# Turning one more head pair's queries and keys by transposing transfers, and loading both heads in one transfer

## The chip, the cores and the metric

The kernel runs on one core of a Trainium2 chip. The metric is the device time in microseconds. Before the change it is 984.49 us, the median of 3 runs (984.35 to 984.61); the profiled execution spans 983.0 us.

## The reference

The computation is a routed attention, and behind it a feed-forward block. There are 4 batches and 8 heads; a head has 768 rows of queries, keys and values with 64 elements each, and 16 centroids.

```python
q_assign = np.argmax(np.einsum('bhsd,hcd->bhsc', q_n, c_n), axis=-1)
k_assign = np.argmax(np.einsum('bhsd,hcd->bhsc', k_n, c_n), axis=-1)
mask = q_assign[:, :, :, None] == k_assign[:, :, None, :]
scores = scale * np.matmul(q, k.transpose(0, 1, 3, 2))
scores = np.where(mask, scores, -1000000000.0)
...
attn_out = np.matmul(softmax(scores), v)
x = attn_out.transpose(0, 2, 1, 3).reshape(B * S, H * D)    # 3072 x 512
out = np.maximum(x @ w_in, 0.0) ** 2 @ w_out                # d_ff = 2048
```

A query attends only to the keys of its own cluster. The norms of queries and keys don't change an argmax, so the kernel leaves them out and normalizes the centroids alone.

## The kernel before

Heads are worked in pairs: pair number 4 b + hp holds heads 2 hp and 2 hp + 1 of batch b, one in partitions 0 to 63 of a turned tile, the other in 64 to 127. There are NG = 16 pairs, HP = 4 to a batch. Each pair has two halves of 384 queries, and each half has six chunks of 128 keys, taken two at a time. So a **unit** is (pair, half, two chunks), three units to a half. The list `units` puts the first halves of pairs 0 to 3 first (units 0 to 11), then the second halves of pairs 0 to 3 (units 12 to 23), then pair by pair both halves of the other twelve pairs (units 24 to 95).

For the scores, queries and keys must lie with the 64 elements of a head along partitions: tile `qkT`, 128 partitions x 12 chunks x 128 columns. There are two ways to get there:

- `turn(pair, part)`, used for pairs 0 to 3: four 128x128 transposes on TensorE (line 256) for each of three parts, each part copied out of PSUM by ScalarE (line 258). The raw tile has both heads of a row side by side, as the transposes need it: [128, 6 chunks, 2 x 64].
- words, used for pairs 4 to 15: `split_words` has ScalarE copy the 32-bit elements as two planes of 16-bit halves into `flat` (line 277, two copies for queries and two for keys), SyncE writes them to DRAM (`words`, line 278), and `turn_words` reads them back with one transposing transfer (line 288) that fills `qkT`.

Behind `qkT` come `logits` (four products with the centroids on TensorE, a copy `lgs` on ScalarE), `route` (three transposes `lt`, then the argmax by five steps on VectorE, lines 340 to 349) and, for pairs of batch 0, `turn_onehot`: the one-hot cluster codes are transposed on TensorE (`po`, line 382) and copied by ScalarE (`ohT`, lines 390 and 392). In batch 0 the mask is added to the scores by products with these one-hot codes (`sc<-ohT`); in other batches VectorE applies it behind the exponential (line 470).

`prep(pair)` is the list of these steps. It is appended to the list `ahead` at the first unit of the pair before (at unit 16 for pair 4), and each unit takes three entries off it; None holds a place. For pairs of batch 0 the list is turn, turn, turn, logits, route, one-hot, one-hot. For the others it begins with `turn_words` and two empty places, and it also holds the two `split_words` steps of the next pair. Pair 4's own split stands at units 12 and 14.

`load_qk` loads queries and keys of a pair: for each of the two, one transfer for each head, on SyncE's queue (for pair 0 the second head's on ScalarE's). A transfer writes pieces of 256 bytes, 768 of them. The pool `loads` with four buffers serves the raw tiles and `flat`. A pair is loaded when `turn(pair - 2, 2)` has been emitted for pairs 2, 3 and 4, and by `split_words` for pairs from 5 on.

In the same stretch of time the two weight matrices are fetched (`w_raw`, 32 transfers of 512 KB, line 139) and rounded in steps of ScalarE, VectorE and GpSimd (lines 150 to 166), four weight pieces for every three units. The products of the feed-forward block for batch 0 (`ph`, `po` with `gT`) are filled in between the units as soon as batch 0's attention is there.

The sums of the exponentials end in `r` (line 551), go to DRAM (`far_r`) and come back to all partitions (`rb`, line 558), where VectorE multiplies them into `xT` (line 570).

Each engine works through its own queue in order. The programming layer orders instructions by priority and its own estimate of when they can run, so a line's place in the program is not always its place in a queue. SyncE's queue holds nearly all transfers: a transfer that must wait holds up all behind it.

Of the kernel before, what the change touches and what calls it, by code (L numbers as in the profile page):

```python
# [8 lines left out]
F32 = mybir.dt.float32  # L9
BF16 = mybir.dt.bfloat16  # L10
I32 = mybir.dt.int32
U16 = mybir.dt.uint16
# [6 lines left out]
P = 128  # L19
# [6 lines left out]
def kernel(  # L26
# [10 lines left out]
    nc = tc.nc  # L37

    B, H, S, D = q.shape
    C = centroids.shape[1]  # L40
    NCH = S // P
# [4 lines left out]
    HP = H // 2  # L46
# [13 lines left out]
    loads = ctx.enter_context(tc.tile_pool(name="loads", bufs=4))  # L60
    loads_v = ctx.enter_context(tc.tile_pool(name="loads_v", bufs=2))
    qktp = ctx.enter_context(tc.tile_pool(name="qktp", bufs=2))
# [9 lines left out]
    qkt_early = early.enter_context(tc.tile_pool(name="qkt_early", bufs=HP - 2, side="right"))  # L72
# [8 lines left out]
    def bank(name, shape):  # L81
        return ps_f.tile(shape, F32, name=name, tag="f")

    def first_bank(name, shape, dtype=F32):

        return ps_av.tile(shape, dtype, name=name, tag="av")

    def together(products, offset=2000):

        products = iter(products)  # L90
        last = nc.tensor.matmul(**next(products))  # L91
        with tc.high_priority(offset=offset):
            for product in products:
                last = nc.tensor.matmul(**product)  # L94
        return last.ins


    raw = {}
    raw_v = {}

    def load_qk(pair):
        if pair >= NG:
            return
        b, hp = divmod(pair, HP)
        raw[pair] = []
        for name, src in (("q_raw", q), ("k_raw", k)):
            t = loads.tile([P, NCH, 2 * D], F32, name=name, tag="qk")
            for e in range(2):
                (nc.scalar if pair == 0 and e else nc.sync).dma_start(
                    t[:, :, D * e : D * (e + 1)],  # L110
                    src[b, 2 * hp + e].rearrange("(p j) d -> p j d", p=P),
                )
            raw[pair].append(t)
# [15 lines left out]
    for fr in range(DFF // NW):  # L129
        for a in range(KT):  # L130
            cols = slice(fr * NW, (fr + 1) * NW)
# [37 lines left out]
    cen = once_early.tile([P, D], F32, name="cen")  # L169
    nc.scalar.dma_start(cen, centroids.rearrange("h c d -> (h c) d"))  # L170
    load_qk(0)
    load_qk(1)

    ident = const.tile([P, P], F32, name="ident")
# [3 lines left out]
    for _ in range(8):  # L178
# [14 lines left out]
        out=odd[:, 1:2], in0=row_i, scalar1=1.0 / C, scalar2=None, op0=ALU.mult  # L193
    )
    constants = nc.vector.tensor_scalar(
        out=odd[:, 0:1], in0=odd[:, 1:2], scalar1=-1.0, scalar2=1.0, op0=ALU.mult, op1=ALU.add
# [48 lines left out]
    qkT = {}  # L245
# [3 lines left out]
    def turn(pair, part):  # L249
        if part == 0:  # L250
            pool = qkt_early if 2 <= pair < HP else qktp
            qkT[pair] = pool.tile([P, 2 * NCH, P], F32, name="qkT")
        pt = bank("pt", [P, 4, P])
        for i in range(4):
            which, c = divmod(4 * part + i, NCH)
            nc.tensor.transpose(out=pt[:, i], in_=raw[pair][which][:, c], identity=ident)
        dst = qkT[pair][:, 4 * part : 4 * part + 4]
        nc.scalar.copy(out=dst, in_=pt)
        if part == 2:
            raw.pop(pair)  # L260
            if pair in (0, 1, HP - 2):
                load_qk(pair + 2)


# [4 lines left out]
    def split_words(pair, which):  # L269
        if which == 0:  # L270
            words[pair] = dram.tile([2 * NCH, P, 2, 2 * D], U16, name="words")
        flat = loads.tile([P, NCH, 2, 2 * D], U16, name="flat", tag="qk")
        src = raw[pair][which].bitcast(U16).rearrange("p c (d two) -> p c two d", two=2)
        half = NCH // 2
        with tc.issue_after(last_exp[0]):
            for cols in (slice(0, half), slice(half, NCH)):
                nc.scalar.copy(out=flat[:, cols], in_=src[:, cols])
        nc.sync.dma_start(
            words[pair][NCH * which : NCH * (which + 1)].rearrange("c p two d -> p c two d"),
            flat,  # L280
        )
        if which == 1:
            raw.pop(pair)
            load_qk(pair + 1)

    def turn_words(pair):
        qkT[pair] = qktp.tile([P, 2 * NCH, P], F32, name="qkT")
        nc.sync.dma_start(
            qkT[pair].rearrange("p c n -> p (c n)").bitcast(U16),
            words.pop(pair).rearrange("c p two d -> (c p two) d"), transpose=True,  # L290
        )
# [4 lines left out]
    def logits(pair):  # L296
        hp = pair % HP
        lg = (bank if pair else first_bank)("lg", [P, TB])
        last_logits[pair] = together(
            dict(  # L300
                out=lg[32 * g : 32 * g + 32], lhsT=cnT[:, 2 * C * hp : 2 * C * (hp + 1)],
                rhs=qkT[pair][:, NB * g : NB * (g + 1)], start=True, stop=True,
            )
            for g in range(4)
        )
        lgs[pair] = once.tile([P, TB], F32, name="lgs")
        nc.scalar.copy(out=lgs[pair], in_=lg)

    def route(pair):
        with tc.high_priority(offset=2000) if pair <= HP else ExitStack():  # L310
            number(pair)
# [51 lines left out]
    def turn_onehot(pair, which):  # L363
        if pair == 0:

            pt = first_bank("po", [P, 2, NB, P], BF16)
            for i in range(2):
                for c in range(NB):
                    nc.tensor.transpose(
                        out=pt[:, i, c], in_=oh[:, c, 2 * i + which].rearrange("p e c -> p (e c)"),  # L370
                        identity=ident_b,
                    )
            dst = qid[pair][1][:, :, TB * which : TB * (which + 1)]
            src = pt.rearrange("p i c n -> p i (c n)")
            nc.vector.tensor_copy(out=dst[:, 0], in_=src[:, 0])
            nc.scalar.activation(
                out=dst[:, 1], in_=src[:, 1], func=ACT.Copy, bias=-BIG, scale=BIG
            )
            return
        pt = ps_f.tile([P, NCH, P], BF16, name="po", tag="f")  # L380
        for c in range(NCH):
            nc.tensor.transpose(
                out=pt[:, c],
                in_=oh[:, c % NB, 2 * which + c // NB].rearrange("p e c -> p (e c)"),
                identity=ident_b,
            )
        dst = qid[pair][1][:, which]
        src = pt.rearrange("p c n -> p (c n)")
        if which == 0:
            nc.scalar.copy(out=dst, in_=src)  # L390
        else:
            nc.scalar.activation(out=dst, in_=src, func=ACT.Copy, bias=-BIG, scale=BIG)

    def spread(pair):

        src, dst = qid[pair]
        n = 4 * NB
        pb = ps_f.tile([n, P], BF16, name="pb", tag="f")
        nc.tensor.transpose(out=pb, in_=src.rearrange("p g e i -> p (g e i)"), identity=ident_b)
        row = once.tile([n, P], BF16, name="row", tag="b")  # L400
        nc.scalar.copy(out=row, in_=pb)
        far = dram.tile([n, P], BF16, name="far")
        nc.sync.dma_start(far, row)
        nc.sync.dma_start(
            dst.rearrange("p g e n -> p (g e n)"),
            far.rearrange("r n -> (r n)").partition_broadcast(P),
        )

    def prep(pair):
        if pair < HP:  # L410
            return [
                lambda: turn(pair, 0), lambda: turn(pair, 1), lambda: turn(pair, 2),
                lambda: logits(pair), lambda: route(pair),
                lambda: turn_onehot(pair, 0), lambda: turn_onehot(pair, 1),
            ]

        split = [lambda i=i: split_words(pair + 1, i) for i in range(2 if pair + 1 < NG else 0)]
        first, second = split or (None, None)
        return [
            lambda: turn_words(pair), None, None, first, None, None,  # L420
            lambda: logits(pair), None, lambda: route(pair), second, None, None,
            None, None, lambda: spread(pair),
        ]
# [367 lines left out]
    for u in range(len(units) + 2):  # L791
        if u < len(units):
            pair, h, c = units[u]
            if (p := next_pair(u)) is not None:
                ahead.extend(prep(p))
            if u in (TWOS, TWOS + 2):

                split_words(HP, int(u > TWOS))
            if c == 0 and u + 3 < len(units) and units[u + 3][0] not in raw_v:
                load_v(units[u + 3][0])  # L800

            with behind_first(u):
                scores(pair, h, c)
# [9 lines left out]
        while v_next < min(ready, len(units)):  # L813
            pair, h, c = units[v_next]
# [19 lines left out]
        while rounding >= 3:  # L834
            rounding -= 3
            i = next(to_round, None)
# [261 lines left out]
```

## Time and profile before

| engine | busy us | share of the span |
| --- | --- | --- |
| TensorE | 962.6 | 98% |
| VectorE | 562.4 | 57% |
| GpSimd | 376.9 | 38% |
| ScalarE | 315.4 | 32% |

Busy time is the time in which an engine worked on an instruction; shares don't add up, since engines work side by side. The DMA engines' mean busy share, in tenths for 40 equal slices of the span, is 9666572534546345452310 and then nothing above 0: they are loaded to about 60% in the first 150 us, to about half until 450 us, and little after. They move 127575 packets, 74.32 MB; 90906 of the packets are under 512 bytes. Of the groups that the change touches, the 24 transposes of queries on TensorE (and as many of keys) take 272 ns each as the median, the 12 copies out of PSUM 591 ns, the 48 copies into `flat` 816 to 857 ns, and a transposing transfer occupies SyncE's queue for 2.6 to 5.3 us.

### The profile page before, as it was taken

The numbers are of one execution on the slowest core, as the hardware profiler recorded it, in microseconds if no ns is written. First come the engines' busy times: TensorE is split into PE (matmuls) and PEld (weight loads), VectorE is DVE, ScalarE is ACT, GpSimd is POOL, SyncE is SP. The second block draws the span as 40 slices with busy tenths as digits, with TensorE's granted clock in tenths as the row PEclk, the third lists the DMA queues.
The fourth block names the chain that finished last, engine by engine and source line by source line (L and its number), as shares of the span: only waits on it lengthen the run. The fifth ranks groups of instructions, "written<-read, shape, count | busy, mean of one in ns | idle before, by whom it ended". The sixth has DMA issues, their size and how long they took to land.

```text
span 983.0 us, 12011 instructions
## 1 busy us (share of the span) xinstructions
PE 962.6 (98%) x4455; PEld 552.8 (56%) x4455; DVE 562.4 (57%) x913; ACT 315.4 (32%) x510; POOL 376.9 (38%) x277
## 2 busy tenths in 40 slices
PE   7999989999999999999999999999999999999997
PEld 4544444443344444443343555888556888556886
DVE  5777778766566665667654865532566531656331
ACT  5886755444445545544231111000111000111000
POOL 1336666655656556565666231002231002231000
PEclk9999999999999999999999999999999999999999
DMA  9666572534546345452310000000000000000000
GB/s 248 199 186 177 164 212 76 136 108 106 135 111 156 98 109 123 111 142 75 74 42 16 15 0 1 11 22 22 11 1 1 21 22 22 1 0 1 22 22 24
DMA packets 127575, 74.32 MB, mean 76 GB/s; under 512 B 90906, under 2 KB 118934, under 8 KB 127510
## 3 DMA queue, kind: packets, MB, share of 16 engines
q1 hardware_dynamic: 125798, 73.06, 28.1%
q8 instruction: 37, 0.61, 0.3%
q10 hardware_dynamic: 1712, 0.43, 0.2%
q14 instruction: 28, 0.23, 0.1%
HBM read 48.07 MB, written 15.86 MB: 65 GB/s over the span
## 4 chain that ended last, share of the span: by engine, by line
PE 81%; DVE 6%; DMA 5%; issue 3%; ACT 1%; POOL 1%; SPq 1%; ACTq 0%; DVEq 0%; POOLq 0%
PE bank L707 22%; PE bank L676 22%; PE po L597 7%; PE ph L584 6%; PE sc L91 6%; PE sc L94 5%; PE av L91 5%; PE av L94 4%; DMA rb<-far_r 3%; DVE w_raw L162 1%; DVE r L551 1%; PE sm L91 1%; DVE ex L470 1%; DMA far_r<-r 1%; POOL w_in L166 1%
## 5 line engine op out<-in xcount | busy, mean ns | idle before, releaser
L482 POOL TENSOR_TENSOR acc<-acc,ex 128x768 f32<-128x768 f32 x112 | 207.1, 1849 | 115.0 <-DVE ex L470 98.4
L470 DVE SCALAR_TENSOR_TENSOR ex<-qid,ids,sc 128x384 f32<-128x384 bf16 x288 | 157.7, 608 | 63.3 <-ACT sc L466 45.6
L466 ACT ACTIVATE sc<-sc 128x768 f32<-128x768 f32 x144 | 108.5, 792 | 162.1 <-PE sc L94 144.6
L94 PE MATMUL sc<-qkT 64*128 64x384 f32 x576 | 153.4, 505 | 0.7
L94 PE MATMUL av<-ex,v_raw 128*64 128x384 f32 x576 | 136.9, 495 | 0.0
L665 POOL TENSOR_TENSOR w_s<-w_in 128x256 f32<-128x256 f32 x24 | 18.3, 762 | 279.9 <-PE bank L707 162.0
L646 DVE TENSOR_TENSOR g<-bank,g 128x384 f32<-128x384 f32 x144 | 77.9, 556 | 81.5 <-PE bank L676 80.5
L707 PE MATMUL bank<-w_out,g 128*128 128x256 f32 x432 | 95.2, 379 | 0.0
L584 PE MATMUL ph<-xT,w_in 128*128 128x384 f32 x256 | 91.8, 498 | 3.3 <-DVE best L341 2.3
L597 PE MATMUL po<-w_out,gT 128*128 128x512 f32 x192 | 92.7, 615 | 0.0
L91 PE MATMUL sc<-qkT 64*128 64x384 f32 x192 | 87.9, 538 | 2.6 <-DVE ex L470 2.6
L707 PEld LDWEIGHTS bank<-w_out,g 128*128 128x128 f32 x432 | 82.1, 190 | 11.8
L646 DVE TENSOR_TENSOR osb<-bank,osb 128x256 f32<-128x256 f32 x54 | 22.1, 423 | 107.6 <-PE bank L707 102.2
L94 PEld LDWEIGHTS sc<-qkT 64*128 64x128 f32 x576 | 65.4, 187 | 28.6 <-issue 6.7
L91 PE MATMUL av<-ex,v_raw 128*64 128x384 f32 x192 | 81.0, 504 | 0.0
L676 PE MATMUL bank<-xT,w_in 128*128 128x384 f32 x192 | 69.9, 487 | 0.0
L676 PE MATMUL bank<-x_t,w_s 128*128 128x384 f32 x192 | 69.8, 486 | 0.0
L676 PE MATMUL bank<-xT,w_s 128*128 128x384 f32 x192 | 69.8, 486 | 0.0
L584 PEld LDWEIGHTS ph<-xT,w_in 128*128 128x128 f32 x256 | 45.6, 189 | 42.7 <-issue 16.0
L94 PEld LDWEIGHTS av<-ex,v_raw 128*64 128x64 f32 x576 | 49.8, 137 | 34.6 <-issue 34.4
L480 POOL TENSOR_TENSOR acc<-ex 128x768 f32<-128x768 f32 x28 | 51.0, 1822 | 46.9 <-DVE ex L470 39.0
L707 PE MATMUL bank<-w_t,g_s 128*128 128x256 f32 x288 | 65.1, 379 | 0.0
(128 smaller groups left out, 1222.8 us busy)
## 6 DMA issues: line engine op xcount, KB each, us to landing
words<-flat SPq DMA_DIRECT2D x24, 384.0 KB
w_raw<-in_moe_w_in_dram SPq DMA_DIRECT2D x16, 512.0 KB
w_raw<-in_moe_w_out_dram SPq DMA_DIRECT2D x16, 512.0 KB
v_raw<-in_v_dram SPq DMA_DIRECT2D x20, 384.0 KB
q_raw<-in_q_dram SPq DMA_DIRECT2D x31, 192.0 KB
k_raw<-in_k_dram SPq DMA_DIRECT2D x31, 192.0 KB
rb<-far_r SPq DMA_DIRECT2D x62, 96.0 KB
out_dram<-osb SPq DMA_DIRECT2D x23, 256.0 KB
```

Source lines behind the costliest of these rows:

```text
L91: last = nc.tensor.matmul(**next(products))
L94: last = nc.tensor.matmul(**product)
L466: last_exp[0] = nc.scalar.activation(out=t[:, 2 * i : 2 * i + 2] if pair < HP else src, in_=src, func=ACT.Exp, scale=SCALE).ins
L470: nc.vector.scalar_tensor_tensor(out=t[:, 2 * i + e], in0=qid[pair][1][:, h, e], scalar=ids[pair][:, ch % NB, 2 + ch // NB, e : e + 1], in ...
L480: nc.gpsimd.tensor_tensor(out=acc[pair, h], in0=t[:, 0:2], in1=t[:, 2:4], op=ALU.add)
L482: nc.gpsimd.tensor_tensor(out=acc[pair, h], in0=acc[pair, h], in1=t[:, 2 * i : 2 * i + 2], op=ALU.add)
L584: nc.tensor.matmul(ph, lhsT=w_in[:, kk, f * P : (f + 1) * P], rhs=xT[b, h][:, kk], start=(kk == 0), stop=(kk == KT - 1),)
L597: nc.tensor.matmul(po, lhsT=gT[f][:, i * P : (i + 1) * P], rhs=w_out[:, f], start=(f == 0), stop=(f == FT - 1),)
L646: nc.vector.tensor_tensor(out=out, in0=bank, in1=to, op=ALU.add)
L665: nc.gpsimd.tensor_tensor(out=s1, in0=a[1][0], in1=a[1][1], op=ALU.add)
L676: nc.tensor.matmul(bank, lhsT=operands[j][0][:, kk], rhs=operands[j][1][:, kk], start=(kk == 0), stop=(kk == H2 - 1),)
L707: nc.tensor.matmul(bank, lhsT=operands[j][0][:, f], rhs=operands[j][1][:, f], start=(f == 0), stop=(f == F2 - 1),)
```

## The change

Pair 3, the last of batch 0, gets its `qkT` by words and a transposing transfer too, and no longer by transposes on TensorE. Its split steps are put into pair 2's `prep`, between routing and one-hot steps; its own `prep` begins with `turn_words` and two empty places. This takes pair 3's transposes and their copies from TensorE and ScalarE.

From pair 3 on no raw tile has to hold both heads of a row side by side, so the raw tile becomes [128, 2 heads, 6 chunks, 64], and one transfer loads both heads of queries, another both heads of keys, in pieces of 1536 bytes. The side-by-side layout is then made by the copies into `flat`, which are split by head in place of by chunk. The loads of pairs 3 to 15 become fewer transfers with longer pieces. The turned tile of pair 3 is still taken from the early pool.

```diff
         for name, src in (("q_raw", q), ("k_raw", k)):
+            if pair > HP - 2:
+                t = loads.tile([P, 2, NCH, D], F32, name=name, tag="qk")
+                heads = src[b, 2 * hp : 2 * hp + 2]
+                nc.sync.dma_start(t, heads.rearrange("h (p j) d -> p h j d", p=P))
+                raw[pair].append(t)
+                continue
             t = loads.tile([P, NCH, 2 * D], F32, name=name, tag="qk")
...
-            if pair in (0, 1, HP - 2):
+            if pair < 2:
                 load_qk(pair + 2)
...
-        src = raw[pair][which].bitcast(U16).rearrange("p c (d two) -> p c two d", two=2)
-        half = NCH // 2
+        src = raw[pair][which].bitcast(U16).rearrange("p e c (d two) -> p e c two d", two=2)
         with tc.issue_after(last_exp[0]):
-            for cols in (slice(0, half), slice(half, NCH)):
-                nc.scalar.copy(out=flat[:, cols], in_=src[:, cols])
+            for e in range(2):
+                nc.scalar.copy(out=flat[:, :, :, D * e : D * (e + 1)], in_=src[:, e])
...
-        qkT[pair] = qktp.tile([P, 2 * NCH, P], F32, name="qkT")
+        pool = qkt_early if pair < HP else qktp
+        qkT[pair] = pool.tile([P, 2 * NCH, P], F32, name="qkT")
...
     def prep(pair):
-        if pair < HP:
-            return [
-                lambda: turn(pair, 0), lambda: turn(pair, 1), lambda: turn(pair, 2),
-                lambda: logits(pair), lambda: route(pair),
-                lambda: turn_onehot(pair, 0), lambda: turn_onehot(pair, 1),
-            ]
         split = [lambda i=i: split_words(pair + 1, i) for i in range(2 if pair + 1 < NG else 0)]
         first, second = split or (None, None)
+        onehot = [lambda: turn_onehot(pair, 0), lambda: turn_onehot(pair, 1)]
+        turned = [lambda: logits(pair), lambda: route(pair)]
+        if pair < HP - 1:
+            turned = [lambda i=i: turn(pair, i) for i in range(3)] + turned
+            return turned + ([first, *onehot, second] if pair == HP - 2 else onehot)
+        if pair < HP:
+            return [lambda: turn_words(pair), None, None, *turned, *onehot]
```

## The prediction

> **What bounds the kernel now.** I read the table of busy time first, then what TensorE waits for, then the stage that the change touches, queue by queue in order of time.
>
> ```profile
> PE 962.6 (98%) x4455; PEld 552.8 (56%) x4455; DVE 562.4 (57%) x913; ACT 315.4 (32%) x510; POOL 376.9 (38%) x277
> ```
>
> ```profile
> PE sc L91 <- DVE ex L470: 2.6, 3, 1.1
> ...
> PE ph L584 <- DVE best L341: 2.3, 1, 2.3
> ...
> PE ph L584 <- DVE xT L570: 0.8, 1, 0.8
> ```
>
> The first fence is the page (busy us, share of the span); the second is the list of waits (us in total, times, longest). TensorE (PE) is the bound: it idles 20 us of 983. So a change that hides transfers or frees another engine has at most these small waits to win, and whatever makes TensorE wait where it did not is lost outright, because its queue is in order and no later stage has idle time to give back.
>
> The stage concerned is the first halves of batch 0 (about 15 to 75 us), where a pair takes 16 us: units 0 to 11 are pairs 0 to 3, three units each. In the timeline of TensorE and ScalarE (start, duration, engine, instruction):
>
> ```profile
> 48.37 0.87 PE L256 MATMUL pt<-ident,q_raw 128*128 128x128 f32 x6
> ...
> 51.21 0.66 PE L256 MATMUL pt<-ident,k_raw 128*128 128x128 f32 x4
> ...
> 62.49 0.49 PE L94 MATMUL sc<-ohT 64*128 64x384 bf16 x4
> ```
>
> ```profile
> 43.98 0.71 ACT L152 ACTIVATE w_raw<-w_raw 128x512 f32<-128x512 uint32 x1
> 44.89 0.80 ACT L390 COPY ohT<-po 128x768 bf16<-128x768 bf16 x1 [0.20 <-PE po L382]
> ...
> 73.14 1.58 ACT L277 COPY flat<-q_raw 128x768 uint16<-128x768 uint16 x2
> ```
>
> The reader is to see pair 3's transposes on TensorE (six at 48.37, two of k behind them, four at 51.21), its first masked scores at 62.49, and that ScalarE had 0.20 us to spare before the one-hot copy of pair 2. The SyncE queue, and windows of the transfers:
>
> ```profile
> 51.21 1.15 SPq L558 DMA_DIRECT2D rb<-far_r  x2
> ...
> 138.09 3.39 SPq L288 DMA_TRANSPOSE qkT<-words  x1
> ...
> 223.28 4.21 SPq L288 DMA_TRANSPOSE qkT<-words  x1
> ```
>
> ```profile
> 130.00:140.00 10.00, 9.27 (x40) 4.23 (x41) 5.47 (x6) 3.57 (x6) 4.58 (x3) 0.83 0.85 223
> ...
> 228.50:229.00 0.50, 0.50 (x2) 0.19 (x1) 0.34 (x1) 0.00 (x0) 0.50 (x1) 1.00 0.81 177
> 229.00:229.50 0.50, 0.50 (x3) 0.19 (x1) 0.00 (x0) 0.00 (x0) 0.50 (x2) 1.00 0.01 1
> ```
>
> The last three columns of a window are granted clock, DMA share and GB/s. The transposing transfer issued at 223.28 keeps the DMA engines busy until 229.0: 5.7 us from issue, of which 4.2 occupy the SyncE queue. In 130 to 140 the clock is 0.83: it follows the 2.28 us wait that ended at 130.73, and costs 10 x 0.17 = 1.7 us more.
>
> **What the Trainium skill says.** DMA: Bandwidth & Descriptors, Latency and other measured facts, gives transposing transfers 261 GB/s; 128 x 1536 x 4 bytes = 786 KB would take 3.0 us (an estimate from the page), the trace shows 5.7, so I use the trace. The same page, Two DMAs through the same engine are not ordered, says that a transfer that reads what an earlier one writes must wait for its completion on the issuing queue; the trace agrees in the 1.7 us that SyncE once waited for words ahead of a transpose. Specifications there asks for pieces of 512 bytes or more for full rate; the q and k loads are 256-byte pieces now (the page counts 90906 packets under 512 B), but the trace shows only 1.2 us of TensorE time waiting for these loads, at the start. TensorE: Matmul & The Clock Gate, Part 1, says that an idle window of about 3.4 us halves the clock; here 2.28 us already brought a slow stretch.
>
> **The change part by part.**
>
> Removed: 12 transposes on TensorE. By starts, 48.37 to 49.40 and 51.21 to 51.80: 1.03 + 0.59 = 1.62 us, on the bound. Three copies L258 of 0.59 us on ScalarE, hidden.
>
> Added on ScalarE: four flat copies; two take 1.58 us from the row above, or 1.45 by starts. The rows become 12 runs of 64; same element count, so I take the same time. The pair for q falls into ScalarE's idle 1.71 us before the exponential at 40.81: nothing. The pair for k is queued directly ahead of pair 2's one-hot copies. These had 0.20 us to spare, so they start 1.45 - 0.20 = 1.25 us later, and TensorE's masked products of unit 6 (46.51 before) with them. This eats 1.25 of the 1.62 us.
>
> Added transfers: two writes of words and one transpose. Here lies the new wait. In the order in which the changed program queues SyncE's instructions, the write of k's words stands behind the two rb transfers, which end at 52.36, and these hang on pair 1's sums, not on anything that the change speeds up. So it issues at about 52.4. A words write alone (458.57) kept the DMA engines busy until 461.0, 2.4 us; under load the one at 133.22 let its transpose start at 138.09, 4.9 us. The transpose thus starts between 54.8 and 57.3 and lands some 6 us later (5.7 above, 6.5 for the one at 466.94 beside a broadcast): between 60.8 and 63.3; I take 62.
>
> Who waits: TensorE's logits of pair 3, which the changed order puts right after pair 2's sums. TensorE gets there at 58.2: unit 6's masked products at 47.76, 1.86 to unit 7, 1.81 and 1.44 for its scores and products with v, 1.82 and 1.44 for unit 8, 2.09 for the sums (all by starts of before). It idles 3.8 us, with everything behind it: pair 3's scores, two products with v, the masked scores. Then comes the routing chain, which before ran beside scores, v products and 2.1 us of sums: logits 0.8, copy 0.6, transposes 0.6, five VectorE steps 3.0 (56.43 to 59.4), one-hot transposes 0.8, two copies 1.5: 7.3 us. Masked scores of unit 9 at 62 + 7.3 = 69.3. Before they came at 62.49 with two products with v still to do, 2 x 1.44: 65.4. Lag 3.9 us (2.7 to 5.2 with the landing); it already contains the saved transposes. The idle time should cost a slow clock: 1.7 us at 130, of which part falls into the chain's own waits; I take 1.2 (0 to 1.7). Sum: +5.1.
>
> Loads of pairs 3 to 15: 26 transfers of 256 packets for 52 of 768. On SyncE two loads took 1.28 us, v_raw, of the new shape, 0.39: 26 x 0.9 = 23 us off a queue that is mostly idle. The rb transfers of the later stage move up by 0.6 us, since no load stands ahead of them. VectorE waits 56.8 us for rb in all, but TensorE only 2.6 us for VectorE in 150 to 500. I take -0.5 (0 to -2.6). TensorE's 0.8 us at 82 for xT should go, as VectorE does pair 3's 384-wide reciprocal at once after a late sum: -0.8. The 2.3 us wait at 128 stays: VectorE's lateness there starts with rb at 111.7, behind a weight load that waits for GpSimd; nothing of that is touched. Placing pair 3's tile in the early pool costs nothing.
>
> **Forecast**: 984.49 + 5.1 - 0.5 - 0.8 = 988.3 us. Chance 0.58.
>
> **Rivals.**
> - *Nearly even* (0.17): the transpose lands at 60.8, lag 2.7, no clock dip, and the later waits give back 0.8 + 1.3: 985.1. For it: a lone words write needs only 2.4 us. Against: weight and k loads are in flight (DMA share 0.66 in 50 to 60).
> - *Faster* (0.20): the wait at the logits is met because the write issues earlier than the SyncE order suggests or its neighbours wait less. Then 1.62 - 1.25 = 0.4 is kept, the 0.8 at 82 and 2.3 of the 2.6 later go: 984.49 - 3.5 = 981.0. For it: these waits exist and the DMA share is 0.5 in 250 to 450. Against: the write would have to issue by 49.8 (58.2 less 6 less 2.4), ahead of sums that end at 44.4 plus reciprocal and two transfers.
> - *Worse* (0.05): SyncE, held 4.2 us by the transpose, also delays v and the next weights, and the stall at 128 grows: 994.
>
> The slow end of the main case is 5.2 + 1.7 = 6.9, 991.4. Range 982 to 992: it leaves out most of the faster case and the worst. Faster by over 0.2% (below 982.5) 0.2; within it 0.17; slower (above 986.5) 0.63.
>
> **What would show it.** TensorE waiting 2.5 to 5 us at pair 3's logits (L91, lg) for a DMA near 58 us, then a clock below 1.0 in 60 to 70; one-hot copies of pair 2 starting about 46.1; the write of k's words near 52.4 and the transpose at 55 to 57; masked scores of unit 9 at 68 to 71; fewer than 60,000 packets under 512 B (90906 less 52 x 768 = 39,936, plus those of one more transpose); no gain over 2.6 us after 150. Wrong if the logits wait under 1 us, or if the 128 us stall vanishes.

## The result, and the profile after

| kernel | median us (lowest to highest) | ratio to before, 95% interval |
| --- | --- | --- |
| before | 984.55 (983.53 to 984.82) | |
| changed | 991.73 (988.48 to 994.27) | 1.0073 [1.0051, 1.0094] |
| changed, a second time (before: 984.29) | 990.2 (988.59 to 991.86) | 1.0063 [1.0045, 1.0082] |

The change makes the kernel slower by about 7 us in one session and 6 in the other; 988.3 was forecast. The profiled execution of the changed kernel is the fastest of the first six, 988.48 us, with a span of 986.7 us against 983.0 before. So its trace shows less of the loss than the median has.

The page, first the busy line of the engines, then the packets:

```profile
PE 963.9 (98%) x4443; PEld 552.1 (56%) x4443; DVE 564.4 (57%) x913; ACT 316.1 (32%) x511; POOL 375.8 (38%) x277
...
DMA packets 98552, 75.89 MB, mean 77 GB/s; under 512 B 53691, under 2 KB 89911, under 8 KB 98487
```

TensorE has 12 instructions less, as it should, and yet is busy 1.3 us longer: a busy TensorE is not one at full clock. Packets under 512 bytes fell from 90906 to 53691. The list of what TensorE waits for (us in total, times, longest):

```profile
PE lg L91 <- DMA qkT<-words: 4.2, 1, 4.2
PE sc L91 <- DVE ex L477: 2.4, 1, 2.4
...
PE ph L591 <- DVE best L347: 2.3, 1, 2.3
...
PE sc L94 <- ACT ohT L398: 0.9, 1, 0.9
```

The first line is the new wait at pair 3's logits, for the transposing transfer. The third is the stall at 128 us, unchanged. The last is pair 2's one-hot copy, late behind the flat copies. The second stands near 472 us, and was not foreseen. TensorE's timeline around the new wait (start, duration, engine, line, instruction, idle time before it):

```profile
46.57 0.50 PE L94 MATMUL sc<-ohT 64*128 64x384 bf16 x4 [0.92 <-ACT ohT L398]
...
54.95 2.16 PE L94 MATMUL sm<-ex,ups 128*32 128x192 f32 x48
...
61.32 0.51 PE L91 MATMUL lg<-qkT,cnT 128*32 128x384 f32 x1 [4.21 <-DMA qkT<-words]
...
63.90 0.90 PE L323 MATMUL lt<-ident,lgs 128*128 128x128 f32 x3
...
69.53 0.84 PE L388 MATMUL po<-ident_b,oh 128*128 128x128 bf16 x12
71.75 0.50 PE L94 MATMUL sc<-ohT 64*128 64x384 bf16 x4
```

The logits start at 61.32 after 4.21 us of nothing; the masked scores of unit 9, which came at 62.49 before, come at 71.75. SyncE's queue shows why the words are late:

```profile
49.52 1.14 SPq L565 DMA_DIRECT2D rb<-far_r  x2
50.76 0.53 SPq L283 DMA_DIRECT2D words<-flat  x1
...
54.94 4.24 SPq L294 DMA_TRANSPOSE qkT<-words  x1
```

The second write of words goes out behind the two rb transfers, and the transfer starts 4.2 us after it, 6.4 us before its data release TensorE. And the windows behind the wait (stretch, length, busy us and counts of PE, PEld, DVE, ACT, POOL, then granted clock, DMA share, GB/s); the last two are cut where the clock changes:

```profile
60.00:65.00 5.00, 3.68 (x15) 1.44 (x17) 1.59 (x3) 0.48 (x1) 1.28 (x1) 0.68 0.98 296
65.00:70.00 5.00, 5.00 (x23) 2.04 (x24) 2.62 (x5) 0.00 (x0) 0.00 (x0) 0.64 0.44 170
...
61.82:68.65 6.83, 6.83 (x23) 2.71 (x17) 2.78 (x5) 0.48 (x1) 0.96 (x1) 0.50 0.77 286
68.65:72.00 3.35, 3.35 (x30) 1.41 (x26) 0.00 (x0) 1.65 (x3) 0.00 (x0) 1.00 0.04 11
```

The two thirds of the first two rows are averages: TensorE runs at half its clock from 61.8 to 68.7, for 6.8 us, and at full clock behind that. In the kernel before, the slow stretch behind the stall at 128 us, which the prediction took its price from, is half as long:

```profile
131.54:134.96 3.42, 3.42 (x11) 1.28 (x12) 1.18 (x3) 0.00 (x0) 1.21 (x1) 0.50 0.29 50
```

In the changed kernel's row from 65 to 70 the busy column of TensorE is full, but only 23 products fall into it; the kernel before had 34.

Where the 3.7 us of the two spans come from, by the starts of units (the first product of queries and keys of each), changed less before:

| stretch | us |
| --- | --- |
| start to unit 4 (a clock of 1.00 against 0.93 in the first 25 us; 0.5 us of waiting for pair 0's keys against 1.0) | -1.0 |
| units 4 to 13, the stage of pair 3 | +7.4 |
| units 13 to 82 | -3.8 |
| units 82 to 86 (near 472 us) | +3.0 |
| unit 86 to the end (a clock of 1.00 against 0.97 from 500 to 550) | -1.9 |

The first and last rows are mostly those of the single executions, not of the change: the clock, and in the first row the arrival of pair 0's keys, whose load is as before. The second execution profiled loses 9.3 in the stage, gains 2.7 in the third stretch and loses 2.9 in the fourth. "Stage" below means units 4 to 13.

### The profile page after: what moved, and what is told of

Read it like the earlier page. It is cut to its first block, busy times and chain, and to the rows that moved or that the text cites. A ratio compares the mean times of both kernels' runs of the same rounds, so it can differ in the third digit from the quotient of the medians.

```text
span 986.7 us, 11955 instructions
## 1 busy us (share of the span) xinstructions
PE 963.9 (98%) x4443; PEld 552.1 (56%) x4443; DVE 564.4 (57%) x913; ACT 316.1 (32%) x511; POOL 375.8 (38%) x277
## 2 busy tenths in 40 slices
DMA packets 98552, 75.89 MB, mean 77 GB/s; under 512 B 53691, under 2 KB 89911, under 8 KB 98487
## 4 chain that ended last, share of the span: by engine, by line
PE 89%; ACT 3%; DVE 3%; DMA 2%; issue 1%; POOL 0%; SPq 0%; ACTq 0%; DVEq 0%; POOLq 0%
PE bank L714 22%; PE bank L683 22%; PE po L604 9%; PE ph L591 7%; PE sc L91 7%; PE sc L94 7%; PE av L91 6%; PE av L94 5%; PE sm L91 1%; ACT ex L473 1%; PE lg L91 1%; DVE w_raw L168 1%; PE sm L94 1%; DMA rb<-far_r 1%; DMA qkT<-words 1%
```

## Experiments

**The two halves of the change.** The first run takes the kernel before and adds only the new loads, for pairs 4 to 15; pair 3 is still turned on TensorE.

```diff
         for name, src in (("q_raw", q), ("k_raw", k)):
+            if pair > HP - 1:
+                t = loads.tile([P, 2, NCH, D], F32, name=name, tag="qk")
+                heads = src[b, 2 * hp : 2 * hp + 2]
+                nc.sync.dma_start(t, heads.rearrange("h (p j) d -> p h j d", p=P))
...
-            for cols in (slice(0, half), slice(half, NCH)):
-                nc.scalar.copy(out=flat[:, cols], in_=src[:, cols])
+            for e in range(2):
+                nc.scalar.copy(out=flat[:, :, :, D * e : D * (e + 1)], in_=src[:, e])
```

> Pair 3 is turned on TensorE as before the change; only the loads of pairs 4 to 15 come as one transfer of 1536-byte pieces for both heads, with the copies into flat split by head. Theory (the loss is TensorE's wait for pair 3's transpose at its logits, 4.2 us, with the unhidden routing and the slow clock behind it; the loads give a little back): no wait at pair 3's logits, up to unit 24 as before, 1 to 3.5 us won from then on, 981 to 983.5 us. Rival (the new loads or the copies by head cost the time, for example by other transfers that they delay): 988 us or more. Second rival (the loads move nothing): 984.5, and the gain after 150 us of the changed kernel came from the shifted timing.

Measured: 981.0 us (978.99 to 985.34), ratio 0.9962 [0.9942, 0.9981]. The stage is untouched (-0.4 us) and units 13 to 82 gain 3.7. Three windows of the kernel before show what was to be had:

```profile
150.00:250.00 100.00, 98.72 (x482) 41.51 (x478) 70.61 (x108) 47.91 (x72) 60.43 (x35) 1.00 0.41 105
250.00:350.00 100.00, 99.19 (x493) 42.28 (x493) 61.27 (x106) 48.10 (x73) 59.64 (x33) 1.00 0.53 128
350.00:450.00 100.00, 99.82 (x510) 43.36 (x512) 61.39 (x107) 51.59 (x80) 60.00 (x34) 1.00 0.47 114
```

TensorE's first column sums to 297.7 of 300, so 2.3 us are idle. With the new loads it is busy throughout:

```profile
150.00:250.00 100.00, 100.00 (x483) 42.39 (x484) 69.40 (x107) 47.83 (x74) 63.22 (x36) 1.00 0.39 108
250.00:350.00 100.00, 100.00 (x500) 43.27 (x498) 62.62 (x108) 48.76 (x75) 60.21 (x34) 1.00 0.47 125
350.00:450.00 100.00, 100.00 (x513) 43.53 (x511) 63.32 (x110) 50.47 (x78) 60.49 (x34) 1.00 0.46 117
```

The gain of 3.7 us is more than the 2.3 us of idle time, but by the starts of units it lies at the same places: the units around these idle times (35, 36, 42, 58 to 60, 64 and 66) are shorter by 3.8 us together, and the others not in sum. The largest wait, in the kernel before and then at the same place with the new loads:

```profile
224.48 0.56 PE L91 MATMUL sc<-qkT 64*128 64x384 f32 x1 [1.14 <-DVE ex L470]
...
224.91 1.53 PE L94 MATMUL sc<-qkT 64*128 64x384 f32 x5
```

```profile
222.23 1.13 PE L94 MATMUL sc<-qkT 64*128 64x384 f32 x5
```

Behind the wait of 1.14 us the next five products take 0.40 us longer at full clock, of which the profile counts 0.14 as idle. So this wait cost more than its entry in the list.

So the loads alone are a gain, and all of the loss belongs to pair 3. The other half confirms it: pair 3 by words, all loads as before and the flat copies by chunk again. Against the changed kernel:

```diff
-            if pair > HP - 2:
-                t = loads.tile([P, 2, NCH, D], F32, name=name, tag="qk")
-                heads = src[b, 2 * hp : 2 * hp + 2]
-                nc.sync.dma_start(t, heads.rearrange("h (p j) d -> p h j d", p=P))
...
-            for e in range(2):
-                nc.scalar.copy(out=flat[:, :, :, D * e : D * (e + 1)], in_=src[:, e])
+            for cols in (slice(0, half), slice(half, NCH)):
+                nc.scalar.copy(out=flat[:, cols], in_=src[:, cols])
```

> Pair 3 by words and a transposing transfer, but all loads in 256-byte pieces, two transfers each, and copies by chunk, as before the change. Theory: TensorE waits 4 to 6 us for the transpose at pair 3's logits, slow clock behind it, no gain from loads: 990 to 994 us. Rival (loads are the cause): within 2 us of before, 983 to 986.

Measured: 996.88 us (991.64 to 997.96), ratio 1.0116 [1.009, 1.0142]; TensorE waits 5.3 us at the logits, the clock is a half from 62.8 to 73.0 us, the stage loses 9.4. That is above the 990 to 994 us that the theory gave. The two halves multiply to 1.0116 x 0.9962 = 1.0078, and the changed kernel's 1.0073 [1.0051, 1.0094] agrees: within the noise the halves add up.

**Is the loss the wait, the clock behind it, or the routing chain?** In the next run, 32 unread products of 128x128 stand directly ahead of pair 3's logits in the changed kernel, so that TensorE does not idle.

```diff
+    def keep_warm(n):
+        scratch = bank("scratch", [P, 4, P])
+        for i in range(n):
+            last = nc.tensor.matmul(
+                scratch[:, i % 4], lhsT=ident, rhs=ex[HP - 2, 0, NCH - 2][:, 0, 0:P],
+                start=True, stop=True,
+            )
+        with tc.issue_after(last.ins):
+            logits(HP - 1)
...
-            return [lambda: turn_words(pair), None, None, *turned, *onehot]
+            return [lambda: turn_words(pair), *[None] * 5, lambda: keep_warm(32), turned[1],
+                    lambda: [step() for step in onehot]]
```

> The changed kernel with 32 products of 128x128 on TensorE put directly ahead of pair 3's logits, into a bank that nobody reads: they only keep TensorE busy while it waits. 32 x 0.12 = 3.8 us at full clock, so they fit into the 4.2 us wait. Theory with the clock as a part of the loss: granted clock 0.95 or more from 60 to 70 us (0.64 to 0.68 in the changed kernel), masked scores of unit 9 some 2.5 us earlier after the landing, 987.5 to 989.5 us and a narrower spread than 988.5 to 994.3. Rival (waits and order alone, the clock doesn't matter): 991 to 993, or later by what the added products overrun.

Measured: 990.36 us (988.58 to 991.36), ratio 1.0058 [1.0037, 1.0079]; the clock is 1.00 from 60 to 70, and the stage still loses 7.5. The time lies between the theory's range and the rival's, and my first reading was that the clock hardly matters. TensorE's timeline says otherwise:

```profile
57.78 7.41 PE L418 MATMUL scratch<-ex,ident 128*128 128x128 f32 x64
65.12 0.51 PE L91 MATMUL lg<-qkT,cnT 128*32 128x384 f32 x1
...
72.52 0.50 PE L94 MATMUL sc<-ohT 64*128 64x384 bf16 x4
```

The 32 products last until 65.19: each takes 0.23 us where 0.12 was expected, and they end some 4 us later than the transfer seems to need (61.3 in the changed kernel). The run had put extra work in the place of the slow clock, and the two came out alike. Half as many products separate them: `keep_warm(16)`.

> The changed kernel with 16 unread 128x128 products directly ahead of pair 3's logits, where the run before it had 32. Those 32 took 7.41 us (57.78 to 65.19, 0.23 each), while the transposed words had landed near 61.2: the logits came 3.9 us later than the transfer asked for, and the stage still lost no more than without the products (7.5 against 7.4 us from unit 6 to unit 13). So the half clock that follows the bare wait must be worth about as much as those 3.9 us. Theory (after the wait the products of the routing chain run at 0.64 to 0.68 of the clock, and that costs 3 to 4 us of the 7.4): 16 products end near 61.5, the clock stays at 1.00 from 60 to 70, the masked scores of unit 9 start at 68 to 69 instead of 71.75, the stage loses 3.5 to 4.5 us, time 986 to 989. Rival (the loss is the routing chain's own waits on VectorE and ScalarE, whatever the clock): masked scores at 71 to 72, stage loss 6.5 to 7.5 us, time 990 to 992.

Measured: 986.02 us (983.25 to 992.41), ratio 1.0018 [0.9993, 1.0043], beside 990.2 for the changed kernel on the same chip. The stage loses 4.1 us. Time, stage and masked scores lie where the theory put them.

```profile
57.07 3.84 PE L418 MATMUL scratch<-ex,ident 128*128 128x128 f32 x32
61.05 0.51 PE L91 MATMUL lg<-qkT,cnT 128*32 128x384 f32 x1
...
66.24 0.84 PE L388 MATMUL po<-ident_b,oh 128*128 128x128 bf16 x12
...
68.45 0.50 PE L94 MATMUL sc<-ohT 64*128 64x384 bf16 x4
```

TensorE is as late at the logits as in the changed kernel (61.05 against 61.32), and nothing is done in those 4 us that anyone reads. But from logits to masked scores it is now 7.4 us, where the changed kernel took 10.4 (11.5 in its second trace, below), with TensorE's products in the same order. So 3 to 4 us of the loss are the clock. The reason is in the two timelines: between the transposes `lt` and `po`, TensorE has scores and products with v to do in order. At full clock VectorE's one-hots, ready at 66.18, set when `po` may start (66.24); at half clock VectorE had them at 67.76 and TensorE came to `po` only at 69.53.

The changed kernel beside it:

> The changed kernel again, beside the three others, to have its spread and its stages on the same chip. Theory: 988.5 to 994, ratio 1.004 to 1.009, a wait of 4 to 4.5 us ahead of pair 3's logits, a clock of 0.62 to 0.7 behind it, 7 to 8 us lost between units 6 and 13, and a wait of 2 to 3 us on VectorE's masks near unit 84. Rival (the stall near unit 84 was a chance of the one execution shown): no wait over 1 us there, 985.5 to 989.

Measured: 990.2 us, with 5.0 us of wait at the logits and 11.5 us from them (62.33) to the masked scores (73.82); the stage loses 9.3. The wait and the loss are more than was expected. Here the half clock lasts from 61.1 to 71.4 us, 10.2 in place of 6.8. The wait near unit 84 is there too (2.5 us).

**Can the transfer come earlier?** The split of pair 3 is moved one unit forward, with the transposing transfer behind it.

```diff
+            if pair == HP - 2:
+                third = turned[2]
+                turned[2] = lambda: (third(), first())
+                return turned + [second, *onehot, lambda: (turn_words(pair + 1), held.append(qkT.pop(pair + 1)))]
...
-            return [lambda: turn_words(pair), None, None, *turned, *onehot]
+            return [lambda: qkT.update({pair: held.pop()}), None, None, *turned, *onehot]
```

> The changed kernel with pair 3's words one unit earlier: the copies of queries join pair 2's third turning step, those of keys stand ahead of pair 2's one-hot steps, and the transposing transfer is emitted at unit 5, not 6. Theory: the transpose lands before TensorE reaches pair 3's logits, no wait there over 1 us and no slow clock, the 1.6 us of transposes and the gain of the loads remain: 980 to 983.5 us. Rival (the transpose's hold on SyncE's queue and the DMA load make weights, values or rb late wherever it stands): 986 us or more, with new waits of TensorE between 45 and 150 us.

Measured: 990.18 us (988.84 to 991.19), ratio 1.0056 [1.0035, 1.0077]: the theory failed, and its rival's 986 us or more with new waits came true. The waits:

```profile
PE lg L91 <- DMA qkT<-words: 2.8, 1, 2.8
...
PE po L388 <- DVE oh L355: 2.2, 1, 2.2
```

TensorE's order had moved too: the logits now stood ahead of unit 8's scores and were reached at 51.4, and a new wait for VectorE appeared. The next run holds the logits where the changed kernel has them, behind pair 2's sums; one unread product enforces it (`keep_warm(1)`, with the same `prep` list as above).

> The split of pair 3 one unit earlier and its transposing transfer issued behind the second write, as in the run with the early split, but the logits are held behind pair 2's sums (one unread product enforces it), so TensorE's order is that of the changed kernel. In the early run the transfer landed at 57.0, just when TensorE comes to the logits in this order (57.0 to 57.8). Theory (the wait for the transfer, with the slow clock that it leaves, is the whole loss of the stage beyond the routing chain): logits wait 0 to 1 us, clock above 0.95 from 55 to 70, masked scores of unit 9 at 65 to 67, loss from unit 6 to unit 13 of 0 to 3 us, time 982.5 to 986.5. Rival (moving the split onto pair 1's and pair 2's first units costs as much, since its transfers hold the weights and its copies the exponentials there): loss already before unit 8, 5 us or more at unit 13, time 989 to 991.

Measured: 991.74 us (991.1 to 992.75), ratio 1.0083 [1.0065, 1.01]. The theory's first half came true: no wait at the logits (57.49). Its time did not. The rival's 989 to 991 us came close, but not its reason: at unit 8 the run is 2.3 us ahead of the kernel before. The loss comes later, by a wait that neither had. On TensorE:

```profile
69.84 1.46 PE L388 MATMUL po<-ident_b,oh 128*128 128x128 bf16 x12 [7.19 <-DVE oh L355]
```

Two rows of VectorE, which is to make these one-hots; eight steps of the weights and a reciprocal between them are left out:

```profile
59.39 0.56 DVE L594 SCALAR_TENSOR_TENSOR xT<-xT,rb 128x384 f32<-128x384 f32 x1 [6.57 <-DMA rb<-far_r]
...
66.75 0.54 DVE L346 TENSOR_REDUCE mx<-lt 128x24 f32<-128x384 f32 x1
```

And SyncE:

```profile
47.66 4.27 SPq L294 DMA_TRANSPOSE qkT<-words  x1
51.99 0.53 SPq L578 DMA_DIRECT2D far_r<-r  x1
...
54.09 1.15 SPq L582 DMA_DIRECT2D rb<-far_r  x2
```

The transposing transfer holds SyncE for 4.27 us just when pair 1's sums want to go to DRAM and back. rb comes late, VectorE stands 6.57 us in front of it in order, the rounding of the weights piles up behind, and routing comes after that. The 7.19 us of idle time on TensorE bring a half clock again, from 67.6 to 74.4 us. The transfer had moved its wait from TensorE's logits to VectorE's queue. The test makes the transfer less early, directly behind rb; its step now stands in pair 3's own `prep`, ahead of the held logits.

```diff
+    last_rb = [None]
...
-                nc.sync.dma_start(rb[D * e : D * (e + 1)], far[e].partition_broadcast(D))
+                last_rb[0] = nc.sync.dma_start(
+                    rb[D * e : D * (e + 1)], far[e].partition_broadcast(D)
+                ).ins
...
+        with tc.issue_after(last_rb[0]):
+            turn_words(HP - 1)
```

> As the run with the early split and held logits, with one instruction moved: the transposing transfer is issued behind the two rb transfers instead of ahead of far_r. There the transfer took SyncE from 47.66 to 51.93, rb came to VectorE at 59.39 after 6.57 us, and VectorE's one-hots 7.2 us late for TensorE. Now rb should go out at 49.5 as in the changed kernel, the transfer at 50.7 to 55.0, landing at 56.9 to 57.1. Theory (the change costs only through its place on SyncE's queue: late, it is waited for, early, it holds rb): logits wait below 0.5 us, no wait over 1 us for VectorE's one-hots, clock above 0.95 from 55 to 70, masked scores of unit 9 at 64.5 to 65.5, a loss of -1 to 1.5 us from unit 6 to unit 13, time 980.5 to 984. Rival (the words of pair 3 cost even without a wait, by their copies and writes under the load of the first 60 us): a loss of 4 us or more, 986 to 990.

Measured: 986.28 us (981.95 to 990.38, 22 runs), ratio 1.0009 [0.9993, 1.0024]. The stage loses 2.6 us, not 9.4.

```profile
59.34 0.51 PE L91 MATMUL lg<-qkT,cnT 128*32 128x384 f32 x1 [0.65 <-DMA qkT<-words]
...
66.26 0.84 PE L388 MATMUL po<-ident_b,oh 128*128 128x128 bf16 x12 [1.83 <-DVE oh L355]
...
68.48 0.50 PE L94 MATMUL sc<-ohT 64*128 64x384 bf16 x4
```

The place on the queue, with the clock that hangs on it (1.00 here from 55 to 75), is worth 5.5 us (991.74 to 986.28; the two ran on the same chip in two sessions, with the kernel before at 984.29 and 985.06). But the theory's 980.5 to 984 was missed, and the time lies in the rival's 986 to 990, though the stage doesn't lose the rival's 4 us or more: waits of 0.65 and 1.83 us are left. Here rb went out at 51.34, which is 1.8 later than in the changed kernel (1.5 of it are the later start of this execution), and VectorE still had weight pieces to round and a reciprocal to do ahead of the routing. The masked scores follow the logits by 9.1 us.

**What makes the gain of the loads?** The run with the new loads alone, but with a transfer for each head again; pieces stay 1536 bytes.

```diff
-                heads = src[b, 2 * hp : 2 * hp + 2]
-                nc.sync.dma_start(t, heads.rearrange("h (p j) d -> p h j d", p=P))
+                for e in range(2):
+                    nc.sync.dma_start(t[:, e], src[b, 2 * hp + e].rearrange("(p j) d -> p j d", p=P))
```

> The run with the new loads alone (pairs 4 to 15 in pieces of 1536 bytes, queries and keys of both heads in one transfer, pair 3 still turned on TensorE: 981.0 us, 0.9962 of the kernel before), but again one transfer for each head, so the pieces stay 1536 bytes and SyncE issues twice as many transfers. Theory (the gain of the new loads comes from the pieces: fewer packets under 512 bytes on the 16 DMA engines): 980.5 to 982, ratio 0.995 to 0.998. Rival (it comes from SyncE's issue time: 1.28 us for two issues, 0.39 for one): 983.5 to 985, ratio 0.998 to 1.001.

Measured: 983.13 us (980.38 to 985.01), ratio 0.9988 [0.9974, 1.0001]. The ratio lies in the rival's range, near its lower end, and the time between the two ranges. Units 13 to 82 gain 1.6 us in its trace, against 3.7 with one transfer for both. Both causes may have a part, but the intervals overlap and don't settle it. The new loads alone once more, on the chip of the run behind rb:

> The new loads alone once more (pair 3 turned on TensorE, pairs 4 to 15 loaded in one transfer of 1536-byte pieces), beside the run before it: it gave 981.0 us, 0.9962. Theory: 979.5 to 982.5, ratio 0.995 to 0.998, the gain spread over units 24 to 72 where SyncE's queue is fullest. Rival (the gain was in part that no wait for VectorE's masks fell near unit 84 in that run, as it did in all others with new loads): with such a wait 982.5 to 984.

Measured: 982.69 us (979.44 to 989.2, 22 runs), ratio 0.998 [0.9967, 0.9994]. The median lies in the rival's range, 0.2 above the theory's. But the profiled execution, which has the wait near unit 84, took 980.26 us and not the rival's 982.5 or more, so neither is confirmed. It is the best version tried, and in both its sessions ahead of the kernel before. Beside 986.28 it also says that pair 3 by words, even with the transfer in its best place tried, costs 3.6 us against TensorE's transposes.

The two profiled executions of this one program show what the +3.0 us near unit 84 is. VectorE and GpSimd in the first:

```profile
460.04 0.95 DVE L623 TENSOR_TENSOR xT<-xT 128x768 f32<-128x768 f32 x1
```

```profile
459.40 5.74 POOL L487 TENSOR_TENSOR acc<-acc,ex 128x768 f32<-128x768 f32 x2 [3.13 <-DVE ex L475]
```

and in the second:

```profile
459.99 2.56 DVE L623 TENSOR_TENSOR xT<-xT 128x768 f32<-128x768 f32 x1
```

```profile
459.35 4.87 POOL L487 TENSOR_TENSOR acc<-acc,ex 128x768 f32<-128x768 f32 x2 [3.14 <-DVE ex L475]
```

The starts agree to 0.05 us. In the first VectorE runs at once and GpSimd's two take 5.74; in the second VectorE's 0.95 us instruction takes 2.56, all behind it in VectorE's queue is 1.6 us later, and TensorE waits 2.5 us for masks where it waited 0.9: units 82 to 86 lose 0.0 us in the first, 2.8 in the second. The Trainium skill, page "SBUF — State Buffer", section "SBUF: two separate sides", says that VectorE with two SBUF inputs contends for one port pair with GpSimd where that reads SBUF too, that whichever starts first has it for the whole instruction, and that the other blocks. The durations fit that; what gave the pair to the one or the other, the recorded starts don't tell, since GpSimd's is 0.64 us ahead in both. All profiled executions but this first one and that of the kernel before have the 2.56 us too (2.57 in one) and lost 1.5 to 3.2 us here: 2.8 to 3.2 in the seven where 3.4 us at half clock followed the wait, 1.5 to 1.8 in the three where it did not. Since one program shows both, these 3 us need not be an effect of the change; whether the kernel before loses them in some executions is open, as it has one trace.

## Why the prediction was right, and where its sizes were off

Slower was the likeliest case at 0.63, by the mechanism that held; 991.73 lies in the stated range, near its slow end, and 3.4 us above the forecast. That it lies inside is in part luck: pair 3 by words alone took 996.88, outside the range, and the loads gave back more than was taken. By its steps:

- **The wait** (right). The write was put at 52.4 behind rb and came at 50.76; the transfer at 54.8 to 57.3 came at 54.94 and released TensorE at 61.3, in the given 60.8 to 63.3. The logits waited 4.2 and 5.0 us (2.5 to 5 given, 3.8 taken).
- **The flat copies ahead of the one-hots** (right in kind): 44.98 where 46.1 was given, since all ran 1.0 us earlier from the start; TensorE lost 0.92 us, 1.25 was taken.
- **The routing chain** (right at full clock): 7.3 us from landing to masked scores were worked out, 7.4 measured with the clock held up.
- **The slow clock** (the mis-sized term): 1.2 us were taken, at most 1.7. The 1.7 is what a window at 0.83 after a wait of 2.28 us gave, and that window holds 3.4 us at half clock (131.5 to 135.0). Behind the longer wait the half clock lasted 6.8 and 10.2 us, twice and three times as long; this the bound left out. Hardly any of it fell into the chain's own waits: TensorE's scores and v products between `lt` and `po` take longer than VectorE at that clock. The chain took 10.4 and 11.5 us, so the term is 3.0 to 4.1. The run with 16 unread products shows it: the chain is 7.4 us there, and the time 986.0 beside 990.2. This is why unit 9's masked scores came at 71.75 and 73.82 instead of 68 to 71.
- **The stage** was to lose 5.1, less 0.8 at 82 us: 4.3. It lost 7.4 and 9.3. With the measured terms the prediction's own sum closes: landing at 61.3 and 7.4 of chain against masked scores at 65.4, less the earlier start of 1.0, is a lag of 4.3, and 3.0 for the clock makes 7.3; for the second trace 62.3, 7.4, 65.4 less 0.8, and 4.1 make 9.2. The wait at 82 is gone, as forecast (no run tests the reason given); the stall at 128 stays, as forecast.
- **The loads** were taken for -0.5 and bounded at -2.6, the listed waits for VectorE. Units 13 to 82 are 2.2 to 4.1 us shorter in the nine traces with one transfer for both heads. The places were right, since the gain lies at these waits; the bound was wrong, since these waits cost more than their idle time. Not all of the gain in a trace need be owed to the loads: without them, pair 3 by words alone is 1.4 us shorter in units 28 to 82 too. "No gain over 2.6 us after 150" held in the changed kernel's two traces only when taken to the end (2.6 and 1.6 us from unit 24 on), with the loss near 472 us in it; up to unit 82 the first gains 3.7.
- **Packets**: 53691 under 512 bytes, below the 60,000 given.
- **Rivals.** The faster one needed the words by 58.2; the runs with an early split show that they can be there, at the price of rb. The nearly even one supposed no dip of the clock. The worse one, SyncE's 4.2 us delaying others, did not occur in the changed kernel, where the stall at 128 didn't grow; its delay is what happened, to rb, when the transfer was moved ahead of rb.

What stays open: how the gain of the loads splits between piece size and issue time, why one wait brings 3.4 us at half clock, another 6.8 or 10.2 and a third none, and what the 2.6 us that are left with the transfer behind rb would need. No variant with the routing put ahead of the weight rounding was run.

## What to carry to other kernels

Moving work from a busy engine to a transfer pays only if its data can be there when the engine arrives; before counting the 1.6 us saved, follow the transfer back through the queue that issues it and ask both what it stands behind and what will stand behind it. A wait of 4 us on TensorE is to be priced with the slow clock behind it, at its full size if the products that follow are in order and on the path, and not by the price of a shorter wait. Test the parts of a change apart: here one half was worth +1.2% and the other -0.2 to -0.4%.

## What the runs showed of the hardware

- TensorE's clock was either full or a half in all twelve traces. Around the end of 4.2 to 5.3 us without a product it fell to a half for 6.8 us (changed kernel) or 10.2 us (its second trace, and pair 3 by words alone); after 2.28 us, in the kernel before, for 3.4 us. With unread products in that gap it stayed at 1.00 from 60 to 70 us. Near 472 us a wait of about 2.5 us was followed by 3.4 us at half clock in seven of ten traces and by none in three.
- The transposing transfer of pair 3, 786 KB, held SyncE's queue for 3.8 to 5.7 us in eight traces (4.24 in the changed kernel), and in the changed kernel its data released TensorE 6.4 us after the issue began. Beside the weight loads it could start 4.2 us after the issue of the 384 KB write that it reads.
- A VectorE instruction of 0.95 us took 2.56 us in another execution of the same program, beside two GpSimd additions that then took 4.87 us in place of 5.74; their starts agreed to 0.05 us, and units 82 to 86 differ by 2.9 us.
- A wait of 1.14 us on TensorE, at full clock, was followed by five products in 1.53 us (0.14 of it counted as idle) that took 1.13 without the wait.
